# Attention and a gated feed-forward on one core: the written-out orders of 32 rounds replaced, with whole-quad exponentials

## The chip, the cores and the metric

The kernel runs on one core of a Trainium2 chip. The metric is the device time of one execution in microseconds (us); before the change it is 1197.77 us, the median of three runs (1197.53 to 1202.79). Engines are named as in the profile: PE is TensorE (matmuls), PEld its loading of weights, DVE is VectorE, ACT is ScalarE, POOL is GpSimd, SP is SyncE, which only issues transfers here.

## The reference

With S = 2048 tokens, D = 448, 16 heads of 28 and F = 1792, all in float32:

```python
qkv = x @ wqkv                                    # q, k, v of 16 heads
p = softmax(q @ k.T * 28 ** -0.5)                 # 2048 x 2048 a head
a = (p @ v) @ wo
gate, up = x @ W_gate, x @ W_up
b = (gate * (gate > 0) * up) @ W_down
g = sigmoid((x * gate_w).sum(-1, keepdims=True))
out = g * a + (1 - g) * b
```

## The kernel before

All orders of instructions are written out by hand. Each engine runs its own instructions in the order in which the program issues them; semaphores hold it where data or a buffer is missing.

There are three stages. The first (to about 137 us) projects x to q, k and v, spills q and k to DRAM and takes the first row maxima. The last (from about 1008 us) projects the attention's output with wo, runs the down projection and combines both. Between them lie 32 *rounds*, the loop at line 740: round v works on head v // 2 and half v % 2 of its keys. The lists of matmuls of the feed-forward's gate and up projections run through the rounds as filler.

A round is a string, one letter for one step, and the loop issues the steps in the order of the letters (lines 745 to 807). The letters are:

- **s**, `score()`, line 298: two matmuls (L306) of keys by queries into a wide PSUM tile of 2 x 512, and one ACT operation that empties it. For half of the 16 pairs of a round (after round 0) the score is final and ACT takes the exponential (L310). For the other half, the *raw* ones, the maximum of these queries isn't known yet: ACT copies the score, negated, to SBUF (L312), and the pair is noted in `todo_max`.
- **b**, `block_min()`, line 240: one DVE minimum (L256) over a raw pair, read from its PSUM tile and the running minimum of its block; the first one of a block reads the copy of the first pair and the tile of the second. Three of them finish a block (512 queries by 1024 keys, two blocks a round).
- **A**, `all_max()`, line 267: DVE reduces a finished block's minimum over the partitions (L271, L265, L275) and spreads it again (L279, `rm`).
- **g**, `take_max()`, line 282: POOL subtracts `rm` from one raw *quad* of 2048 elements a partition (L285); four a round.
- **e**, `take_exp()`, line 288: ACT takes the exponential of half a raw quad, 1024 elements (L296); eight a round. The dictionary `halves` remembers which half is next.
- **P** and **Q**, `pv()`, line 645: the product of the round's probabilities with v, 32 matmuls each on a tile of 32 columns (L653). P needs the first half of the round's keys, Q the second. After Q of an even round ACT copies the sum (L659), after Q of an odd one DVE adds to it (L661), and the row sums are sent to be inverted.
- **m**, `smax()`, line 190: two matmuls (L200) for the row maxima of a head to come, and a DVE reduction (L204) that empties the tile. **n**, line 208, turns a head's maxima into a row of Q (L212 and after).
- **x**: one matmul (L600) of the gate or up projection; 11 make a unit, and after a unit ACT takes the relu (L610) or DVE multiplies and SP stores (L613, L619).
- **w**: ACT and POOL split half of a gate/up weight tile in a high and a low part; SP loads the next.
- **c**, **f**: in odd rounds the two parts of `rescale()` (line 627), with DVE, ACT and POOL (L637, L640, L641). **N**: `normalise()` (line 677), POOL's multiplication with the inverted sums of the head before (L679) and four stores on SP. **D**: the split of a down-projection tile in the last rounds. **l**, **u**: once, in round 0.

s, m and n also start transfers and small steps: the first and the ninth s of an even round load k and q of a later head, the sixth calls `small_things` (lines 746 to 751).

s and m take their wide PSUM tiles in turn from three (`ps_w`, line 110): the fourth fill needs the first tile empty, that is the copy or exponential done, for raw pairs but the first of a block also the minimum, for m the reduction. The probabilities live in ten quads of SBUF (`NP`), and four pairs of the next round are scored ahead.

Before the change the list is `FIRST, A1`, then `Ee, Oe` three times, `A8`, then `O, E` ten times, and `L5, L6, L7`; E-type strings stand in even rounds, O-type in odd ones.

Of the kernel before, what the change touches and what calls it, by code (L numbers as in the profile page):

```python
# [42 lines left out]

NP = 10

FIRST = "sbbsbAxxxxlusxgxsxxsxssxsxxxsxxsesxxxxbegxxseexwPbbAQ"

A1 = "smsxxxswbxxxsgbsbnxxxxxssxssxxsAxemxwxmgxsmxxmcessxxxsmxsxbxeggxxxxxesebxeefbewxmmNAwPQ"

Ee = "gswmwsxxxxbsxgsxsxxbebxxxsxxssxxAxssxxemxxxmxsmxeexgmxxsexmxmxxsemxxxsgsbesbbewAwPQ"  # L50

Oe = "sgmgwsxxxxbssxxxsxbxxbxnsxsxsxsAwsxmxxemxxsmxeemsegwxmxxxxmsmxxgexNxsxsbesbxexbcwefxPAQ"

A8 = "wwwsmsxxsxxxxbsxbxgsexxsbxxxxsssxxgxxsAxmxmexxsxemxxgxmsxmexxmsxmxexxgessbbesPewbAQ"

O = "ssbnsxxxxsxbxNxbxxggsxxxxsxxxsxsxxssxxAmxsxxemsxmxexxmxsmxxemmgexsbxxxsbcxxxsbxAxmgeePefeQ"

E = "gsmsxxxxssebxxbbxxxsxxxxmxAexxssxgsxxsxxsxxmxxsxxemsmexgxexmxxxmsxmxexsbxsgebsebAPQ"

L5 = "sxsbNxxssxbxbxxxnxxxgssxxxegxxxAsxxsxgsxsxsxxxxxscsesxxxgxxxxxexxxxxeexsxeexxxsebbbfxxPAQ"  # L60

L6 = "DsxxsgxxxbsbxxgxssxxsxbexexxsAssxsxxxssxxxxexxxxgsgxxxexxxsxssexxebxexDbbxxxexPAQ"

L7 = "ssssxxxxxbxgxbxxxebxxxxxxgxxesxAxsexexxsgsxxxsxxxxgsxxxxxexesNexexxxcxDsxxxPfDQ"

ROUNDS = [
    FIRST, A1, Ee, Oe, Ee, Oe, Ee, Oe,
    A8, O, E, O, E, O, E, O,
    E, O, E, O, E, O, E, O,
    E, O, E, O, E, L5, L6, L7,  # L70
]


# [11 lines left out]
def gated_mix_kernel(ctx, tc, x, wq, wo, wgu, wd, out):  # L85
# [8 lines left out]
    def f32(ap):  # L94
        return ap.bitcast(F32)
# [21 lines left out]
    def ps_x(name):  # L117
        return psum.tile([P, TB], F32, tag="x", bufs=2, name=name)
# [71 lines left out]
    def smax(k):  # L190

        h, u, half = maxima[k]
        full = 4 * rows_of(h).count(2)
        if u == 0 and half == 0:
            MX[h] = keep.tile([P, 2 * full], F32, name=f"mx_{h}", tag="mx", bufs=2)
            M[h] = keep.tile([P, NU[h]], F32, name=f"m_{h}", tag="m", bufs=2)
        ps = ps_w(f"sm_{k}")
        for c in range(2):
            k0 = (half * 2 + c) * TB
            nc.tensor.matmul(ps[:, c, :], Q[h][:, u * P:(u + 1) * P], K[h % 3][:, k0:k0 + TB],  # L200
                             start=True, stop=True)
        c = 2 * u + half
        to = MX[h][:, c:c + 1] if u < full else M[h][:, u:u + 1]
        nc.vector.tensor_reduce(to, ps, axis=AX.XY, op=OP.max)  # L204
        if c == 2 * full - 1:
            nc.vector.tensor_reduce(M[h][:, :full], MX.pop(h).rearrange("p (a b) -> p a b", b=2), axis=AX.X, op=OP.max)
# [12 lines left out]
    AT, QUAD, slots = {}, {}, iter(range(10 ** 6))  # L219
# [18 lines left out]
    RM, R2, left = {}, {}, {}  # L238
# [46 lines left out]
        nc.gpsimd.tensor_tensor(QUAD[q], QUAD[q], m, op=OP.subtract)  # L285
        todo_exp.append(q)

    def take_exp():
        q = min(todo_exp, key=lambda q: (q[0], q[2], -q[1]))
        k = halves.pop(q, 0)  # L290
        if k:
            todo_exp.remove(q)
        else:
            halves[q] = 1
        q = QUAD[q][:, 2 * k:2 * k + 2].rearrange("p c t -> p (c t)")
        nc.scalar.activation(q, q, AF.Exp, scale=-SCALE)  # L296

    def score():

        v, done, q, half, chunks = stream.pop(0)  # L300
        h = v // 2
        if q not in QUAD:
            QUAD[q] = p_slot(next(slots) % NP, f"P_{v}_{q[1]}_{q[2]}")
        ps = ps_w(f"s_{v}_{chunks[0][0]}_{chunks[0][1]}")
        for c, (k, j) in enumerate(chunks):
            nc.tensor.matmul(ps[:, c], K[h % 3][:, k * P:(k + 1) * P], Q[h][:, j * TB:(j + 1) * TB], start=True, stop=True)  # L306
            AT[v, k, j] = QUAD[q][:, 2 * half + c]
        dst = QUAD[q][:, 2 * half:2 * half + 2]
        if done:
            nc.scalar.activation(dst, ps, AF.Exp, scale=SCALE)  # L310
        else:
            nc.scalar.activation(dst, ps, AF.Copy, scale=-1.0)  # L312
            todo_max.append((v, chunks[0][1], dst, ps if v else None))
# [275 lines left out]
    def load_f(i):  # L589
        if NF <= i < NB * NF:  # L590
            WS[i] = fe.tile([P, 2, 7, P], F32R, name=f"wg_{i}", tag="wg", bufs=2)
            nc.sync.dma_start(f32(WS[i]), ws_d[i % NF])
# [103 lines left out]
    def early_d():  # L696

        for i in range(0, 4, 2):
            h = fe.tile([P, 2, 4, P], F32, name=f"hk_{i}", tag="wgr", bufs=2).rearrange("p s c f -> p (s c f)")
            for k in range(2):  # L700
                DR[i + k] = V[:, 0].rearrange("p k h d -> p (k h d)")[:, (i + k) * D:(i + k + 1) * D]
                HK[i + k] = h[:, k * TB:(k + 1) * TB]
                nc.sync.dma_start(DR[i + k], wd[(i + k) * P:(i + k + 1) * P])
                nc.sync.dma_start(HK[i + k], h_d[i + k])
# [13 lines left out]
    def small_things(u):  # L718

        h, q = divmod(u, 4)  # L720

        if u in (22, 38):
            g = 2 if u < 32 else 3
            nc.sync.dma_start(V[:, g % 2], v_d[g])
        if u == 1:
            gates()
        if u == 2:
            pack_wo()
        if h and q == 1:
            row_sums(h - 1)  # L730
            spread(h - 1)

    def loads(h, load):

        if 2 < h + 2 < H:
            load(h + 2)
# [3 lines left out]
    for v, order in enumerate(ROUNDS):  # L740
        small_things(2 * v)
        if v == 2 * H - 3:
            early_d()
        ns = 0
        for o in order:
            if o == "s":
                ns += 1
                if ns == 6:
                    small_things(2 * v + 1)
                if ns in (1, 9) and v % 2 == 0:  # L750
                    loads(v // 2, load_k if ns == 1 else load_q)
                if stream:
                    score()
            elif o == "m":
                if m < len(maxima):
                    smax(m)
                    m += 1
            elif o == "x":
                i, half, n = passes.pop(0)
                if n == 0:  # L760
                    units.append((i, half, ps_x(f"gu_{i}_{half}")))
                gu_mm(units[-1][2], i, half, n)
                if n == NT - 1:
                    i, half, ps = units.pop()
                    if half:
                        finished.add(i)
                        load_f(i + 2)
                    spill_h(i, ps) if half else relu(i, ps)
            elif o == "n":
                if v % 2 and v < 2 * H - 1:  # L770
                    smax_end(v // 2 + 1)
            elif o == "w":
                ready = -(-starts[v + 2] // NT)
                ready = min(ready + ready % 2, 2 * NF)
                while parts < ready and (parts < 4 or parts // 2 - 2 in finished):
                    split_f(parts // 2, act_high, pool_low, (parts % 2,))
                    parts += 1
                    if parts % 2 == 0:
                        fetch_f(parts // 2 + 1)
            elif o == "b":  # L780
                block_min()
            elif o == "A":
                all_max()
            elif o == "g":
                take_max()
            elif o == "N":
                if v > 1 and v % 2:
                    normalise(v // 2 - 1)
            elif o == "e":
                take_exp()  # L790
            elif o in "cf":
                rescale(v, "cf".index(o))
            elif o == "D":
                split_wd(len(early))
                early.append(o)
            elif o == "l":
                sends.pop()()
            elif o == "u":
                split_f(0, act_high, pool_low, (1,))
                QS.append(last_q("Q2"))  # L800
                for a, b in ((GD, 12), (GD + 12, 4)):
                    nc.sync.dma_start(f32(QS[2])[a:a + b].rearrange("p j t -> p (j t)"), Q[1][GD + 2:GD + 2 + b].bitcast(F32))
                load_q(2)
                fetch_f(2)
                parts = 2
            elif o in "PQ":
                pv(v, "PQ".index(o))
        rest = [k for k in todo_exp + todo_sub + todo_all if k[0] == v]
        assert not rest and v not in PO or len(stream) == max(0, 16 * (2 * H - 1 - v) - AHEAD), (v, passes, rest, len(stream) + 16 * (v + 1))
# [178 lines left out]
```

## Time and profile before

| | us |
|---|---|
| median of three runs | 1197.77 |
| lowest and highest | 1197.53, 1202.79 |
| span of the profiled execution (first to last instruction) | 1198.9 |
| granted TensorE clock | 1.000 |

The profiled execution's own time isn't given beside its span; the span is 1.1 us above the median.

| stretch, us | PE | DVE | ACT | POOL |
|---|---|---|---|---|
| 207.80 to 235.32 (one early round) | 27.31 | 24.23 | 26.06 | 23.12 |
| 371.43 to 923.47 (20 rounds) | 552.02 | 488.28 | 484.73 | 401.31 |
| 923.47 to 949.58 | 25.94 | 16.52 | 23.11 | 19.16 |
| 949.58 to 976.61 | 25.41 | 15.32 | 25.38 | 21.83 |
| 1047 to 1199 | 148.27 | 55.43 | 32.87 | 23.37 |

How to read it: busy times are unions of the instructions' spans on an engine. Matmuls are pipelined and their ends are modelled, so PE counts as busy in short waits too; what it lost is seen in the chain that ended last, where its pieces have start and length. A group of instructions has its line, engine, operation, output and input with their shapes, the count, then busy time and mean ns of one, then the idle time of the engine just before them and what ended it.

### The profile page before, as it was taken

Reading aid. Unit: us, or ns where it says so; the run is one execution under the profiler, and the core shown is the slowest. Engines: PE = TensorE matmul, PEld = TensorE weight load, DVE = VectorE, ACT = ScalarE, POOL = GpSimd, SP = SyncE. Lnnn points to the kernel's source line nnn. Section 1 sums busy time; section 2 is a strip of 40 time slices with the busy share of each in tenths; the row PEclk is TensorE's granted clock in tenths of the full one; section 3 lists DMA queues with packets and bytes.
Section 4 is the critical chain, followed back from the end, with each engine's and each line's share of the span. In section 5 each row is a group of like instructions: output and inputs, shape, how many; then the busy total and the mean of one; then the engine's idle time right before and its main releaser. Section 6 shows DMA issues by size and latency. Waiting matters only on the chain.

```text
span 1198.9 us, 16948 instructions
## 1 busy us (share of the span) xinstructions
PE 1183.7 (99%) x6183; PEld 820.1 (68%) x6183; DVE 902.8 (75%) x1179; ACT 878.2 (73%) x1082; POOL 748.9 (62%) x326
## 2 busy tenths in 40 slices
PE   9999999999999999999999999999999999999998
PEld 6888755556656666666666666666666666899997
DVE  6466798888898989898888989898988653544242
ACT  5321789999999888888788888888888896422121
POOL 4222387889897777766676767777767786522020
PEclk9999999999999999999999999999999999999999
DMA  9956354354535453443536443436443425743342
GB/s 317 319 207 250 136 191 137 111 141 143 156 129 159 148 163 114 124 122 117 150 119 186 118 129 110 128 117 191 112 126 105 138 89 161 218 136 119 114 128 75
DMA packets 63486, 178.35 MB, mean 149 GB/s; under 512 B 13050, under 2 KB 19650, under 8 KB 58754
## 3 DMA queue, kind: packets, MB, share of 16 engines
q1 hardware_dynamic: 56812, 151.53, 41.1%
q0 software_dynamic: 6160, 25.30, 5.5%
q8 instruction: 48, 0.79, 0.3%
q10 hardware_dynamic: 432, 0.46, 0.1%
q14 instruction: 34, 0.28, 0.1%
HBM read 118.58 MB, written 58.87 MB: 148 GB/s over the span
## 4 chain that ended last, share of the span: by engine, by line
PE 85%; DVE 5%; ACT 3%; DMA 3%; issue 1%; POOL 1%; SPq 1%; DVEq 0%; POOLq 0%; ACTq 0%
PE gu L600 19%; PE s L306 18%; PE po L653 18%; PE sm L200 10%; PE acc L893 10%; PE qk L427 6%; PE wo L852 3%; PE v L445 3%; DVE r L256 1%; ACT P L310 1%; DVE mx L204 1%; ACT P L312 1%; ACT P L296 1%; DMA ls<-os 1%; DMA wor<-wo_d 1%
## 5 line engine op out<-in xcount | busy, mean ns | idle before, releaser
L285 POOL TENSOR_TENSOR P<-P,rm 128x2048 f32<-128x2048 f32 x102 | 470.7, 4633 | 95.5 <-DVE rm L279 79.7
L600 PE MATMUL gu<-X,wg 128*128 128x512 f32 x1232 | 364.6, 395 | 0.7 <-ACT rl L610 0.7
L204 DVE TENSOR_REDUCE mx<-sm 128x1 f32<-128x1024 f32 x256 | 301.5, 1215 | 40.9 <-PE sm L200 40.5
L306 PE MATMUL s<-Q,K 128*128 128x512 f32 x1024 | 316.8, 405 | 6.2 <-ACT V L310 1.9
L600 PEld LDWEIGHTS gu<-X,wg 128*128 128x128 f32 x1232 | 231.2, 188 | 56.7 <-ACT rl L610 2.0
L306 PEld LDWEIGHTS s<-Q,K 128*128 128x128 f32 x1024 | 178.1, 188 | 98.5 <-DVE mn L265 13.4
L312 ACT ACTIVATE P<-s 128x1024 f32<-128x1024 f32 x204 | 202.9, 1031 | 44.2 <-PE s L306 41.6
L653 PE MATMUL po<-P,V 128*32 128x512 f32 x1640 | 227.7, 594 | 0.4 <-ACT P L296 0.4
L296 ACT ACTIVATE P<-P 128x1024 f32<-128x1024 f32 x204 | 213.2, 1072 | 2.1 <-POOL P L285 1.8
L310 ACT ACTIVATE P<-s 128x1024 f32<-128x1024 f32 x206 | 201.5, 1039 | 9.0 <-PE s L306 7.7
L256 DVE SCALAR_TENSOR_TENSOR r<-s,r 128x1024 f32<-128x1024 f32 x124 | 151.6, 1223 | 19.0 <-ACT P L312 10.5
L200 PE MATMUL sm<-K,Q 128*128 128x512 f32 x520 | 163.7, 399 | 0.7 <-DVE mx L204 0.6
L653 PEld LDWEIGHTS po<-P,V 128*32 128x32 f32 x1640 | 63.5, 110 | 116.3 <-issue 108.8
L653 PE MATMUL po<-V 128*32 128x512 f32 x408 | 135.9, 594 | 0.0
L285 POOL TENSOR_TENSOR V<-V,rm 128x2048 f32<-128x2048 f32 x24 | 111.1, 4634 | 23.0 <-DVE rm L279 19.3
L121 ACT ACTIVATE hh<-hr 128x512 fp32r<-128x512 f32 x52 | 32.8, 631 | 117.9 <-PE acc L893 111.8
L200 PEld LDWEIGHTS sm<-K,Q 128*128 128x128 f32 x520 | 91.3, 188 | 33.2 <-ACT P L310 5.6
L127 DVE TENSOR_TENSOR hh<-hr,hh 128x512 fp32r<-128x512 f32 x52 | 47.8, 926 | 82.6 <-ACT hh L121 78.9
L893 PE MATMUL acc<-WD,hh 128*128 128x448 f32 x480 | 100.7, 368 | 0.0
L893 PEld LDWEIGHTS acc<-WD,hh 128*128 128x128 f32 x480 | 90.1, 188 | 8.8
L256 DVE SCALAR_TENSOR_TENSOR r<-s,P 128x1024 f32<-128x1024 f32 x50 | 61.1, 1223 | 38.3 <-ACT P L312 38.3
L271 DVE TRANSPOSE_TENSOR_REDUCE mn<-r 128x32 f32<-128x1024 f32 x63 | 78.0, 1238 | 1.3
(87 smaller groups left out, 1142.6 us busy)
## 6 DMA issues: line engine op xcount, KB each, us to landing
wg<-ws_d SPq DMA_DIRECT2D x42, 896.0 KB
K<-qk_d SPq DMA_DIRECT2D x32, 448.0 KB
Q<-qk_d SPq DMA_DIRECT2D x64, 224.0 KB
h_d<-h SPq DMA_DIRECT2D x56, 256.0 KB
hr<-h_d SPq DMA_DIRECT2D x52, 256.0 KB
ws_d<-wg SPq DMA_DIRECT2D x14, 896.0 KB
qk_d<-st POOLq DMA_DIRECT2D x21, 512.0 KB, 3.2
wgr<-wgu SPq DMA_DIRECT2D x13, 512.0 KB
```

The costliest lines, as they stand in the source:

```text
L200: nc.tensor.matmul(ps[:, c, :], Q[h][:, u * P:(u + 1) * P], K[h % 3][:, k0:k0 + TB], start=True, stop=True)
L204: nc.vector.tensor_reduce(to, ps, axis=AX.XY, op=OP.max)
L256: nc.vector.scalar_tensor_tensor(r, ps, -1.0, before, op0=OP.mult, op1=OP.min)
L271: nc.vector.tensor_reduce(MN[:, 1:3], R2.pop((v, j)).rearrange("p a (b r) -> p a b r", r=32), axis=AX.X, op=OP.min, apply_transpose=True)
L285: nc.gpsimd.tensor_tensor(QUAD[q], QUAD[q], m, op=OP.subtract)
L296: nc.scalar.activation(q, q, AF.Exp, scale=-SCALE)
L306: nc.tensor.matmul(ps[:, c], K[h % 3][:, k * P:(k + 1) * P], Q[h][:, j * TB:(j + 1) * TB], start=True, stop=True)
L310: nc.scalar.activation(dst, ps, AF.Exp, scale=SCALE)
L312: nc.scalar.activation(dst, ps, AF.Copy, scale=-1.0)
L600: nc.tensor.matmul(ps, WS[i][:, s, a], xf(i // NF, b), start=(n == 0), stop=(n == NT - 1))
L653: nc.tensor.matmul(po[32 * j:32 * j + 32], V[:, h // 4 % 2, k, h % 4], AT.pop((v, k, j)), start=(k == k0), stop=(k == k0 + NK // 2 - 1))
L893: nc.tensor.matmul(ACC[i // NF][t][:, :D], HH[i][:, a, t * P:(t + 1) * P], wd_high_low(f, b), start=(f == 0 and n == 0), stop=(f == NF - 1 ...
```

## The change

The sixteen orders R0 to R12 and R29 to R31 replace the ten before. Round 0 keeps its string. Rounds 1 to 8 get an order each; rounds 9 to 28 repeat R9, R10, R11, R12; the last three are new. A new letter E takes the exponential of a whole raw quad in one ACT operation of 2048 elements; e still takes half. In the list of rounds each b stands later behind the s of its pair than before, on the mean.

```diff
@@ -43,31 +43,43 @@
 
 NP = 10
 
-FIRST = "sbbsbAxxxxlusxgxsxxsxssxsxxxsxxsesxxxxbegxxseexwPbbAQ"
-
-A1 = "smsxxxswbxxxsgbsbnxxxxxssxssxxsAxemxwxmgxsmxxmcessxxxsmxsxbxeggxxxxxesebxeefbewxmmNAwPQ"
-
-Ee = "gswmwsxxxxbsxgsxsxxbebxxxsxxssxxAxssxxemxxxmxsmxeexgmxxsexmxmxxsemxxxsgsbesbbewAwPQ"
-
-Oe = "sgmgwsxxxxbssxxxsxbxxbxnsxsxsxsAwsxmxxemxxsmxeemsegwxmxxxxmsmxxgexNxsxsbesbxexbcwefxPAQ"
-
-A8 = "wwwsmsxxsxxxxbsxbxgsexxsbxxxxsssxxgxxsAxmxmexxsxemxxgxmsxmexxmsxmxexxgessbbesPewbAQ"
-
-O = "ssbnsxxxxsxbxNxbxxggsxxxxsxxxsxsxxssxxAmxsxxemsxmxexxmxsmxxemmgexsbxxxsbcxxxsbxAxmgeePefeQ"
-
-E = "gsmsxxxxssebxxbbxxxsxxxxmxAexxssxgsxxsxxsxxmxxsxxemsmexgxexmxxxmsxmxexsbxsgebsebAPQ"
-
-L5 = "sxsbNxxssxbxbxxxnxxxgssxxxegxxxAsxxsxgsxsxsxxxxxscsesxxxgxxxxxexxxxxeexsxeexxxsebbbfxxPAQ"
-
-L6 = "DsxxsgxxxbsbxxgxssxxsxbexexxsAssxsxxxssxxxxexxxxgsgxxxexxxsxssexxebxexDbbxxxexPAQ"
-
-L7 = "ssssxxxxxbxgxbxxxebxxxxxxgxxesxAxsexexxsgsxxxsxxxxgsxxxxxexesNexexxxcxDsxxxPfDQ"
+R0 = "sbbsbAxxxxlusxgxsxxsxssxsxxxsxxsesxxxxbegxxseexwPbbAQ"
+
+R1 = "smNsxsxbxsxwbxbwnxxgsxxxwxsgAwxsxssxxsxsmxExxmxxmxxssxgxmsxxbsbcxexxxexmsPbgAmEemfexQ"
+
+R2 = "gwsmsxsxbxswxxxxxxbExbxsxsxxmAxsxsxsxgxxxsmxxsxmExmgsxxgmxxsxmxExsssewxbbePwbmAQ"
+
+R3 = "smgsxsxbxwxbswxxxsxxxxsbxwAxsswxxxggsmnxgxsxemxsmxxssmxexEmxxxmxxsbxNxssxEebbcePfAmxQ"
+
+R4 = "gwsmsxxsxbsxxxxxbexwxsbxssmxsgAxxssxxsxmxsexxxmgsmxxxxmmgwsxxxEExxsexxsbxmebbAPwQ"
+
+R5 = "smsxsxggxxsxwbbxbnxAsxxxxsxssxsxwsxEwmxxgmxxmxsxxxxsmsExmxxmsxxxesxsNcbbegebfAPemwxxQ"
+
+R6 = "smsxxbgsxsxxxwbxxsxbwxssssAgxsxmxxxsxxmxExmxsxxmsgEmxxmxxxEgxxmxssxsbPbewxbexwAQ"
+
+R7 = "ngsmsxxxssNxbxxxsxxxwbbxsxxsssxwsexxAxmxxxmswgxxsxgmsxmexgmsxxsebbxxxsxxemPEbecfeAxmQw"
+
+R8 = "swmssxbxwxxsbxbxxsxxsgxwExxxmsxmxsxxxgAsxxssxmsxxmxsemxxmsxgxExgxxsbxmbsbeeewxAPQ"
+
+R9 = "nsmsbxxxgsxxbsbxxxsxxxxsxxgsxxAsxxsmsNxxxsmsxxsmsxxsxxxxbbxmxxEmgxxEgsxxxmbxcEAeexfxmPQ"
+
+R10 = "smsxxgxxssbbbxxxxxxExxmxsxxsxxxsxxAsxxxsmsxxxgsmsxEmxxmggsxExmxxmsxsbxxexbsebAPQ"
+
+R11 = "nsmsbxxxsxbxxsxbxxAxsgxxsgxxssxxsxsxgxmxsxxmxsmxxxEmxsxmExExmxxmxxxNcxxxsgssbbefxxebPAQ"
+
+R12 = "smsbgxxxxssxxxxxsbxxxxbAxxessxgxsxsxxsxmxexxmxsmxxsmxxmgxEmsgxxxxmxxEssxebbsePbQA"
+
+R29 = "NgsxsbsxbxxxxsbnxxsxxxsxAxxxExxgxxsxsgsxsxxxxxsxxxsxxxxsxEsbExxsgxcxesxxxxexxfbPbAQ"
+
+R30 = "DsxxsxsxxsgxxxbsxbxbxxsxxxxEAxgsxgsxxxxxsxxxsxxsxsxxxssxExxbxsxxxEgxsexxxDexxbxxbPQA"
+
+R31 = "sxNxsbxsxxgxxxbssxxxxbxsxAxexsxsexgxxExxxxxxgxsexxgxxxexsxxsxxcexxexsDfDPxQ"
 
 ROUNDS = [
-    FIRST, A1, Ee, Oe, Ee, Oe, Ee, Oe,
-    A8, O, E, O, E, O, E, O,
-    E, O, E, O, E, O, E, O,
-    E, O, E, O, E, L5, L6, L7,
+    R0, R1, R2, R3, R4, R5, R6, R7,
+    R8, R9, R10, R11, R12, R9, R10, R11,
+    R12, R9, R10, R11, R12, R9, R10, R11,
+    R12, R9, R10, R11, R12, R29, R30, R31,
 ]
 
 
@@ -285,14 +297,14 @@
         nc.gpsimd.tensor_tensor(QUAD[q], QUAD[q], m, op=OP.subtract)
         todo_exp.append(q)
 
-    def take_exp():
+    def take_exp(whole):
         q = min(todo_exp, key=lambda q: (q[0], q[2], -q[1]))
         k = halves.pop(q, 0)
-        if k:
+        if k or whole:
             todo_exp.remove(q)
         else:
             halves[q] = 1
-        q = QUAD[q][:, 2 * k:2 * k + 2].rearrange("p c t -> p (c t)")
+        q = QUAD[q][:, 2 * k:4 if whole else 2 * k + 2].rearrange("p c t -> p (c t)")
         nc.scalar.activation(q, q, AF.Exp, scale=-SCALE)
 
     def score():
@@ -786,8 +798,8 @@
             elif o == "N":
                 if v > 1 and v % 2:
                     normalise(v // 2 - 1)
-            elif o == "e":
-                take_exp()
+            elif o in "eE":
+                take_exp(o == "E")
             elif o in "cf":
                 rescale(v, "cf".index(o))
             elif o == "D":
```

## The prediction

> **What bounds the kernel now.** I read the page first: the busy shares, then the chain that ended last.
>
> ```profile
> span 1198.9 us, 16948 instructions
> ...
> PE 1183.7 (99%) x6183; PEld 820.1 (68%) x6183; DVE 902.8 (75%) x1179; ACT 878.2 (73%) x1082; POOL 748.9 (62%) x326
> ...
> PE 85%; DVE 5%; ACT 3%; DMA 3%; issue 1%; POOL 1%; SPq 1%; DVEq 0%; POOLq 0%; ACTq 0%
> ```
>
> TensorE looks full, but the ends of matmuls are modelled, so a matmul that waits a little for its PSUM tile still counts as busy. The question is therefore how much of the span TensorE would need if no matmul waited. For that I read the chain in order of time, at whole P-V blocks (po, 64 instructions), which come once a round, and the times of undisturbed matmuls between them.
>
> ```profile
> 180.07 7.00 PE po L653 x64
> ...
> 371.43 7.00 PE po L653 x64
> ...
> 923.47 7.00 PE po L653 x64
> ...
> 943.99 3.27 PE gu L600 x14
> ...
> 949.58 7.27 PE po L653 x64
> ...
> 976.61 7.30 PE po L653 x64
> ```
>
> ```profile
> 574.78 0.92 PE s L306 x4
> ...
> 599.23 1.14 PE s L306 x4
> 600.37 0.11 PE mt L212
> ```
>
> A 512-column matmul takes 3.27/14 = 0.233 us, a round's P-V block 7.00. The four matmuls straight behind a block take 1.14 instead of 0.92: the turn from a block to other work costs 0.2 us, whatever the order. The first and the last block, and the end, are read from the timeline of TensorE:
>
> ```profile
> 149.11 3.83 PE L653 MATMUL po<-P,V 128*32 128x512 f32 x31
> ...
> 1000.85 5.44 PE L653 MATMUL po<-P,V 128*32 128x512 f32 x48
> ...
> 1007.41 0.60 PE L653 MATMUL po<-P,V 128*32 128x512 f32 x2
> ...
> 1046.42 0.68 PE L852 MATMUL wo<-WO,on 128*128 128x448 f32 x2 [1.76 <-POOL on L130]
> ```
>
> Now count letters between one block and the next (s and m are two matmuls, x is one, and the mt of 0.11 comes every second round) and subtract.
>
> Block 0 to 1: 81 matmuls and a block are 18.9 + 7.0 = 25.9; it took 180.07 - 149.11 = 31.0. **Lost 5.1.**
> Blocks 1 to 8: 7 x (25.9 + 0.06) = 181.5; it took 191.4. **Lost 9.9**, of it 7 x 0.2 = 1.4 for the turns.
> Blocks 8 to 28: ten pairs of 88 and 85 matmuls, 54.4 a pair, 544.2; it took 552.0. **Lost 7.8**, of it 4.0 for the turns.
> Blocks 28 to 31: 79 + 73 + 68 = 220 matmuls, 51.3 + 21 = 72.3; it took 77.4. **Lost 5.1**, of it 0.6 for the turns.
> After block 31 TensorE runs on and waits once, 1.76 us ahead of the output projection.
>
> So an order without any wait could save about 4.9 + 8.5 + 3.8 + 4.5 + 1.8 = 23.5 us, and no order more. What holds TensorE is the three wide PSUM tiles that s and m share: the fourth fill waits until ScalarE or VectorE has emptied the first. How full those are:
>
> ```profile
> 235.32:262.38 27.06, 26.76 (x149) 16.61 (x153) 24.88 (x34) 25.12 (x31) 25.14 (x12) 1.00 0.55 151
> 262.38:289.97 27.59, 27.35 (x150) 16.33 (x154) 24.23 (x32) 26.25 (x35) 22.67 (x10) 1.00 0.35 126
> ...
> 371.43:923.47 552.04, 552.02 (x3025) 353.30 (x3028) 488.28 (x645) 484.73 (x550) 401.31 (x123) 1.00 0.44 132
> ```
>
> (In the view by windows the columns are the length, then PE, PEld, DVE, ACT, POOL.) In the early rounds ScalarE works 25.1 to 26.3 of 27.1 to 27.6 us, as much as TensorE needs (25.9): two engines of equal load and a third (VectorE, 24.2 to 24.9) close behind. From round 9 on the shares are 88% for both, and the loss is small.
>
> **The change, part by part.** TensorE's work is the same: each letter but e occurs as often as before in the whole list, and 79 E take the place of 158 e. Three x leave round 29 and three leave round 31, six go to round 30.
>
> *Whole exponentials.* Their price comes from these groups:
>
> ```profile
> L310 ACT ACTIVATE P<-s 128x1024 f32<-128x1024 f32 x206 | 201.5, 1039 | 9.0 <-PE s L306 7.7
> L296 ACT ACTIVATE P<-P 128x1024 f32<-128x1024 f32 x204 | 213.2, 1072 | 2.1 <-POOL P L285 1.8
> L256 DVE SCALAR_TENSOR_TENSOR r<-s,P 128x1024 f32<-128x1024 f32 x50 | 61.1, 1223 | 38.3 <-ACT P L312 38.3
> L121 ACT ACTIVATE hh<-hr 128x512 fp32r<-128x512 f32 x52 | 32.8, 631 | 117.9 <-PE acc L893 111.8
> L121 ACT ACTIVATE WO<-wor 128x1344 fp32r<-128x1344 f32 x1 | 1.3, 1309 | 0.0
> ```
>
> From 512 to 1344 elements an ACTIVATE grows by (1309 - 631)/832 = 0.815 ns an element, so one of 2048 is estimated at 1072 + 1024 x 0.815 = 1.91 us. No trace here shows one. Against two halves that is 0.24 us less; where ScalarE runs without a gap two halves take only 1.89 (the row x2 below), and the saving is 2 x 0.945 - (0.945 + 0.835) = 0.11. So 0.11 to 0.24 per E: 79 E free 9 to 19 us of ScalarE, 17 E in rounds 1 to 8 two to four. The Trainium skill (ScalarE: Activation LUTs, What ACT_TABLE_LOAD costs) gives an ACTIVATE with immediate operands 186 ns and 0.833 ns an element, back-to-back ones overlapping by 93 ns; by that each E would free 0.09 to 0.19 us, 7 to 15 in all, and the halves' 1072 here lie 33 ns above its figure. It counts on TensorE only where ScalarE is what it waits for.
>
> ```profile
> 144.08 4.24 DVE e L556
> 148.63 4.25 DVE gate L558
> ...
> 300.05 1.72 ACT P L312 x2
> ...
> 304.80 3.76 ACT P L310 x4
> ...
> 310.90 1.89 ACT P L296 x2
> 312.79 0.93 ACT V L310
> ```
>
> That is so in the early even rounds: this chain stays on ScalarE from 300.05 to 313.72, because the repeated order piles four half exponentials onto the copies.
>
> *Minima behind their copies.* The row of r<-s,P shows VectorE standing 38.3 us before 50 minima, waiting for ScalarE's copy, with the maxima (m) queued behind. By the letters a minimum follows its fill by 0.47 us of TensorE work in rounds 9 to 28, less than the 1.04 of the copy; in the new orders by 0.82, in rounds 1 to 8 by 1.42 instead of 1.03. So VectorE does maxima in that time and frees m's tiles earlier. Against it, the tile of the copied pair is held as long as before. Worth between nothing and the waits of m's tiles, which are part of the losses above.
>
> *Own orders, rounds 1 to 8.* Block 0 to 1: the gates' two operations of 4.24 and 4.25 us on VectorE stand in round 0, which keeps its order, so I take 1.0 of 4.9. Blocks 1 to 8: between none and all of 8.5; I take half, 4.2, because ScalarE's load stays near TensorE's. Rounds 1 to 3 and 5 to 7 put m or x between P and Q: the last exponentials get time, but each makes one more turn, 6 x 0.2 = 1.2. Net 3.0.
>
> *Rounds 9 to 28.* Half of 3.8: 1.9.
>
> *Rounds 29 to 31.* The chain shows both minima in the way:
>
> ```profile
> 957.61 1.95 ACT P L312 x2
> ...
> 959.59 1.24 DVE r L256
> ...
> 962.19 0.73 PE s L306 x2
> ...
> 1003.24 1.25 POOL os L679
> ...
> 1007.43 1.29 POOL os L641
> ...
> 1008.74 0.70 DVE os L661
> ```
>
> Round 30 now has 79 matmuls instead of 73 ahead of its block and ScalarE has 3 E in each of 29 and 30: I take 2.5 of 4.5. In round 31 N stood behind the last subtraction, so the normalisation of head 14 (1.25) ran ahead of the rescaling (1007.43) for which head 15's addition (1008.74) waited. Now N comes third. The addition can then start at the end of Q, 1008.0: 0.7 us, all of it inside the 1.76 that TensorE waits later.
>
> *Queues.* N moves also its four stores on SP, w its weight loads, the sixth and ninth s their loads of Q and V. The DMA share of rounds 9 to 28 is 0.44, which covers them; a late load of gate/up weights would cost one unit's wait, under 2 us.
>
> **Sum.** 1.0 + 3.0 + 1.9 + 2.5 + 0.7 = 9.1 us. The profiled span is 1198.9, already 1.1 above the median of 1197.77 (the page gives no more of its own time), so the difference is taken from the median: **1188.7 us**.
>
> **Rivals.** *All waits go:* 23.5 - 1.2 = 22.3, 1175.5. For it: every loss is a wait for a tile, and no engine alone exceeds 26.3 us a round. Against: three engines at 90 to 97% in the early rounds would have to fit without a gap. Between it and the forecast lies 1176 to 1182; chance 0.11.
>
> *The waits only move:* the early rounds are set by ScalarE and VectorE together, and a smoother order runs into the other queue; the gain of rounds 1 to 8 is eaten by the extra turns, rounds 9 to 28 give nothing, and half of the last rounds' 3.2 remains: 1196. Chance 0.24.
>
> *E holds up the copies, slower:* ScalarE works in order, so a copy behind an E starts up to 1.91 - 1.07 = 0.84 later. It decides where the copy's tile is refilled within 1.91 + 1.04 = 2.95 us of the E; by the letters that is so at 3 of 79, by 0.2 us each, if ScalarE comes to the E without a backlog. With the backlog of 300 to 314 it is so at each of the 17 E of rounds 1 to 8: +14.3, against 5.1 from the other rounds: 1207. The Trainium skill (TensorE: Matmul & The Clock Gate, Architectural detail) calls ScalarE's queue strict first-in first-out, eight deep, while TensorE may only pull weight loads ahead; by that rule no copy gets past an E. The trace agrees, the chain of ACT above being in the order of the letters. Chance 0.13.
>
> **How the numbers follow.** Forecast 0.52, all waits gone 0.11, moved 0.24, held up 0.13. A measurement here can tell 0.5%, 6 us: faster below 1191.8, slower above 1203.8. Faster 0.52 + 0.11 = 0.63, same 0.24, slower 0.13. The range reaches down to the bound of the sum, 1176, and up through most of "moved" to 1200, leaving out what lies in "held up".
>
> **What would show it.** Blocks 0 to 8 (the blocks themselves move by a few letters) in 218 us instead of 222.3, 8 to 28 in 550, 28 to 31 in 75, the output projection's wait near 1.0; L296 with 79 instructions of about 1.9 us; VectorE's idle time before r<-s,P well below 38. The forecast is wrong if rounds 1 to 8 don't shorten (then ScalarE's load, not its order, bounds them), or if s waits for ACT behind a whole exponential.

## The result, and the profile after

The changed kernel takes 1212.26 us (median of four runs, 1210.45 to 1216.61), the one before 1197.85 beside it: ratio 1.0118, 95% interval 1.009 to 1.0145. It is **slower by 14 us**, 1.2%; the prediction was 1188.7, with 1176 to 1200 as its range. The profiled execution took 1211.34 us, its span is 1209.6. Of the runs below, one execution of e9 (1445.76 us) and one of e15 (4134.21 us) were far slower than the others of their kernels; they are in no ratio, and their profiles are not used.

The page of the profile after, beside the rows of before in the prediction:

```profile
span 1209.6 us, 16837 instructions
...
PE 1188.0 (98%) x6183; PEld 824.0 (68%) x6183; DVE 912.5 (75%) x1179; ACT 878.1 (73%) x1003; POOL 749.3 (62%) x326
...
PE 85%; DVE 6%; DMA 4%; ACT 2%; issue 1%; POOL 1%; SPq 1%; DVEq 0%; POOLq 0%; ACTq 0%
...
L268 DVE SCALAR_TENSOR_TENSOR r<-s,P 128x1024 f32<-128x1024 f32 x50 | 61.1, 1223 | 31.2 <-ACT P L324 31.0
```

ScalarE has 79 instructions fewer and the same busy time (878.1 after 878.2), and of the chain's shares DMA's grew from 3% to 4% and DVE's from 5% to 6%, while ACT's fell from 3% to 2%. One per cent is 12 us, about the size of the difference, but the shares are whole per cents and don't say which of them it is. Where the time went is read from the chain in order of time, at the same P-V blocks as before (block k is the one of round k; line numbers after are those of before plus 12):

```profile
180.11 3.57 PE po L665 x32
...
376.66 7.00 PE po L665 x64
397.78 5.71 DMA X<-x_d
407.04 7.00 PE po L665 x64
...
600.10 7.00 PE po L665 x64
621.71 5.77 DMA X<-x_d
631.04 7.00 PE po L665 x64
...
845.66 5.13 DMA X<-x_d
...
936.80 7.00 PE po L665 x64
```

The chain of before had no piece of DMA between blocks 8 and 28. Now a load of X stands in three rounds, 9, 17 and 25, and those last 30.4, 30.9 and 30.3 us from block to block (407.04 - 376.66 is the first), while the same string takes 28.2 in rounds 13 and 21. The first and last blocks, from TensorE's timeline:

```profile
148.77 1.54 PE L665 MATMUL po<-P,V 128*32 128x512 f32 x11
...
1013.36 3.21 PE L665 MATMUL po<-P,V 128*32 128x512 f32 x28 [0.96 <-ACT rl L622]
...
1058.76 0.67 PE L864 MATMUL wo<-WO,on 128*128 128x448 f32 x2 [1.08 <-POOL on L142]
```

| us, profiled execution | before | after | forecast |
|---|---|---|---|
| blocks 0 to 8 | 222.3 | 227.9 | 218 |
| blocks 8 to 28 | 552.0 | 560.1 | 550 |
| blocks 28 to 31 | 77.4 | 76.6 | 75 |
| block 31 to the end | 198.1 | 196.2 | 197.3 |
| wait of the output projection | 1.76 | 1.08 | near 1.0 |

The spans differ by 10.7 us: -0.3 up to block 0, +5.6 in the early rounds, +8.1 in the steady ones, -0.8 in the last and -1.8 after them. (The medians differ by 14.4: beside the span there are 1.7 us in the profiled execution, which lies 0.9 below its median, while the span of before lies 1.1 above its own.) Both kernels have 648 matmuls of s, m and x between blocks 0 and 8, and equally many between 8 and 28; the last three rounds have one fewer. What stands behind block 31 differs from run to run: in other profiles with the same last rounds it took 195.5 to 201.3 us, so the -1.8 there says little.

### The profile page after: what moved, and what is told of

It reads as the page before. It is cut to its first block, busy times and chain, and to the rows that moved or that the text cites. A ratio compares the mean times of both kernels' runs of the same rounds, so it can differ in the third digit from the quotient of the medians.

```text
span 1209.6 us, 16837 instructions
## 1 busy us (share of the span) xinstructions
PE 1188.0 (98%) x6183; PEld 824.0 (68%) x6183; DVE 912.5 (75%) x1179; ACT 878.1 (73%) x1003; POOL 749.3 (62%) x326
## 4 chain that ended last, share of the span: by engine, by line
PE 85%; DVE 6%; DMA 4%; ACT 2%; issue 1%; POOL 1%; SPq 1%; DVEq 0%; POOLq 0%; ACTq 0%
PE gu L612 19%; PE po L665 18%; PE s L318 17%; PE acc L905 10%; PE sm L212 9%; PE qk L439 6%; PE wo L864 3%; DVE r L268 3%; PE v L457 3%; DMA X<-x_d 1%; ACT P L324 1%; DMA l_d<-rq 1%; DMA or<-o_d 1%; DVE mx L216 1%; DMA ls<-os 1%
## 5 line engine op out<-in xcount | busy, mean ns | idle before, releaser
L216 DVE TENSOR_REDUCE mx<-sm 128x1 f32<-128x1024 f32 x256 | 305.4, 1218 | 54.7 <-PE sm L212 53.0
L318 PE MATMUL s<-Q,K 128*128 128x512 f32 x1024 | 321.8, 404 | 6.0 <-DVE mx L216 2.4
L318 PEld LDWEIGHTS s<-Q,K 128*128 128x128 f32 x1024 | 181.9, 188 | 86.8 <-DVE r L268 17.1
L308 ACT ACTIVATE P<-P 128x1024 f32<-128x1024 f32 (+1 forms) x140 | 201.8, 1459 | 2.0 <-POOL P L297 1.7
L268 DVE SCALAR_TENSOR_TENSOR r<-s,r 128x1024 f32<-128x1024 f32 x124 | 151.8, 1225 | 21.4 <-ACT P L324 10.2
L212 PEld LDWEIGHTS sm<-K,Q 128*128 128x128 f32 x520 | 93.8, 188 | 34.1 <-DVE mx L216 4.4
L268 DVE SCALAR_TENSOR_TENSOR r<-s,P 128x1024 f32<-128x1024 f32 x50 | 61.1, 1223 | 31.2 <-ACT P L324 31.0
```

The costliest lines, as they stand in the source:

```text
L268: nc.vector.scalar_tensor_tensor(r, ps, -1.0, before, op0=OP.mult, op1=OP.min)
```

## The experiments

The rows of before and after suggest a first theory. Here are TensorE's waits by what they wait for (total, times, longest), and around the first reload of X the queues of SP and POOL and TensorE's timeline, all after:

```profile
PE gu L612 <- DMA X<-x_d: 4.6, 6, 1.3
```

```profile
390.14 2.43 SPq L616 DMA_DIRECT2D X<-x_d  x4
394.69 1.61 SPq L693 DMA_DIRECT2D o_d<-os  x4
396.40 1.76 SPq L616 DMA_DIRECT2D X<-x_d  x4
```

```profile
384.19 9.22 POOL L297 TENSOR_TENSOR P<-P,rm 128x2048 f32<-128x2048 f32 x2
393.37 1.29 POOL L691 TENSOR_TENSOR os<-os,rb 128x512 f32<-128x512 f32 x1
```

```profile
403.54 0.73 PE L612 MATMUL gu<-X,wg 128*128 128x512 f32 x2 [1.29 <-DMA X<-x_d]
```

The tokens that the feed-forward works on change three times, at x number 308, 616 and 924, each the 22nd x of an R9, and X is then loaded anew in eight transfers (L616). N stands in the middle of them. Its four stores (L693) wait on SP for POOL's multiplication (L691), which waits for two subtractions of 4.6 us that were issued ahead of it. SP issues in order, so the last four loads of X wait as well: 2.1 us from 392.57 to 394.69 with nothing issued, then 1.6 for the stores. Before, N came earlier, POOL was free for it, and the loads went out in one piece behind the stores:

```profile
383.36 1.70 SPq L681 DMA_DIRECT2D o_d<-os  x4
385.17 4.30 SPq L604 DMA_DIRECT2D X<-x_d  x8
```

**Theory Q**: transfers held up on SP cost most of the loss. **Rival E**: the whole exponentials hold up copies. **Rival O**: the new orders are slower in themselves, by waits for tiles.

The ratios below are against all executions of the kernel before that had been collected by then (medians 1198.87 to 1200.28), so equal times of two runs needn't have equal ratios.

### N behind the reload; whole exponentials as halves

e1 moves one letter of R9, e2 replaces E by ee in every string.

```diff
-R9 = "...smsNxxxsmsxxsmsx..."
+R9 = "...smsxxxsmsxNxsmsx..."
```

```diff
-R2 = "...mxEx...", and so on
+R2 = "...mxeex...", and so on
```

> The changed kernel with the N of R9 moved seven letters later, behind the 22nd x, so that all eight transfers that reload X are issued ahead of the four stores of the normalisation. Theory 'SP queue' (stores wait for POOL until 393.4 and hold the second half of the reload): rounds 9, 17 and 25 fall from 30.4, 30.9 and 30.3 us between blocks to the 28.2 of rounds 13 and 21, the kernel from 1212 to about 1205. Rival 'slow landing' (the letters between last and next use, 4.4 to 6.5 us, are too few for 5.2 us of transfer in any order): these rounds stay above 29.5, the kernel above 1209.

> The changed kernel with each E written as ee, two half exponentials at the same place. Theory 'E holds up the copies': faster by 5 us or more, 1207 or less. Theory 'SP queue': the exponentials' size is not what lost time; within 3 us of 1212, rather above it by what ScalarE loses in rounds 1 to 8 (17 times 0.1 to 0.24, 2 to 4 us).

e1: 1206.68 us, ratio 1.0046 (1.0024 to 1.0068): by the ratios one letter takes back 0.7 of the 1.2%, by the medians 5.6 of the 14.4 us. Its profiled execution ran at a clock of 0.949, so its blocks are compared with each other, an R9 without a reload (488.30) and one with it (600.23), in its chain:

```profile
488.30 7.32 PE po L665 x64
516.81 7.32 PE po L665 x64
...
600.23 7.32 PE po L665 x64
628.72 7.32 PE po L665 x48
```

28.51 and 28.49: the reload now costs nothing. e2: 1212.95, 1.0107 (1.007 to 1.0144), no different from the change. The interval is wide, but the traces agree: blocks 1 to 8, where E was to hold up the copies at 17 places, take 196.5 us with E and with ee. So E is no cause, and no gain that these runs can show, though its price was as estimated (after, groups of one shape):

```profile
L308 ACT ACTIVATE P<-P 128x2048 f32<-128x2048 f32 x64 | 122.1, 1918 | 0.1
```

### The parts of the change alone; the cause put into the kernel before

e3, e4 and e5 take from the change only rounds 9 to 28, 1 to 8 and 29 to 31. e7 is the kernel before with N moved into the reload:

```diff
-O = "ssbnsxxxxsxbxNxbxxggsxxxxsxxxsxsxxss..."
+O = "ssbnsxxxxsxbxxbxxggsxxxxsxxxsxsxNxss..."
```

> The kernel before with R9 to R12 in rounds 9 to 28, and its own orders elsewhere. Theory 'SP queue': three reloads at 2.2 to 2.8 each, plus 1 for the rest: 1197.9 + 8 = 1206. If the loss were the new early rounds' late start that runs through the steady ones: 1199 or less.

> The kernel before with R1 to R8 in rounds 1 to 8, and its own orders elsewhere. By the traces blocks 0 to 8 take 227.8 instead of 222.3: 1197.9 + 5.5 = 1203.4. If the parts didn't add (backlog handed over to rounds 9 and on): above 1206.

> The kernel before with R29 to R31 in its last three rounds. By the traces blocks 28 to 31 take 76.6 instead of 77.5 and TensorE's wait ahead of the output projection 1.1 instead of 1.8: 1 to 2 us faster than the kernel before, 1196 to 1197. The prediction's term for it was 3.2.

> The kernel before with one letter moved: the N of its odd order O goes from behind the 6th x to behind the 18th, between the first four and the last four transfers that reload X in rounds 9, 17 and 25. Theory 'SP queue': these three rounds lengthen by 1.5 to 3 us each, the kernel by 5 to 9; rounds 11, 13, 15 and so on, which have the same N and no reload, stay within 0.3. Rival 'slow landing' or any other property of the new orders: no change.

| kernel | us | ratio (interval) | blocks 0-8 | 8-28 | 28-31 |
|---|---|---|---|---|---|
| e3, rounds 9 to 28 | 1207.68 | 1.0067 (1.0046 to 1.0089) | 222.0 | 559.0 | 77.4 |
| e4, rounds 1 to 8 | 1205.59 | 1.0045 (1.0028 to 1.0062) | 225.9 | 553.6 | 77.5 |
| e5, rounds 29 to 31 | 1198.71 | 0.9996 (0.9984 to 1.0009) | 222.2 | 552.3 | 76.7 |
| e7, before with N in the reload | 1210.59 | 1.0098 (1.0068 to 1.0129) | 222.3 | 563.2 | 77.5 |

The three parts add up: 0.67% + 0.45% - 0.04% is 1.08%, against 1.18% for all. (In e4, 1.5 us of the 553.6 are a wait for X in round 9.) And e7 makes the kernel before slower by nearly as much, with no new order at all. Its SP queue and its waits:

```profile
384.71 2.26 SPq L604 DMA_DIRECT2D X<-x_d  x4
390.96 1.61 SPq L681 DMA_DIRECT2D o_d<-os  x4
392.67 1.76 SPq L604 DMA_DIRECT2D X<-x_d  x4
```

```profile
PE gu L600 <- DMA X<-x_d: 7.1, 3, 3.1
```

Here SP stood 4.0 us. Rounds 9, 17 and 25 took 30.5, 32.7 and 31.6 instead of 28.0; the other odd rounds kept their 27.9 to 28.4. That is 11.2 us for blocks 8 to 28, more than the 5 to 9 expected: in rounds 17 and 25 the granted clock was 0.50 for 3.4 us behind the wait for X (619.8 to 623.2 and 845.1 to 848.4), which costs 1.7 us each time, and without that it is 7.8. For the reloads theory Q is shown from both sides.

### The early rounds: loads of Q and the row sums

In an even round the sixth s issues the row sums (VectorE's reciprocal, L680, a store of it, four loads that spread it) and the ninth s the load of Q behind them, all on SP. In the new strings both stand closer to heavy transfers. After (round 4):

```profile
250.19 0.34 SPq L597 DMA_DIRECT2D ws_d<-wg  x1
...
253.42 0.45 SPq L681 DMA_DIRECT2D l_d<-rq  x1
261.49 2.19 SPq L687 DMA_DIRECT2D rb<-l_d  x4
...
264.41 3.36 SPq L187 DMA_DIRECT2D Q<-qk_d  x4
```

```profile
271.94 0.70 PE L212 MATMUL sm<-K,Q 128*128 128x512 f32 x2 [0.80 <-DMA Q<-qk_d]
```

```profile
307.90 0.25 DVE L680 RECIPROCAL rq<-ls 128x16 f32<-128x16 f32 x1 [1.87 <-DMA ls<-os]
```

The store of the row sums is small, but SP could read it back only 8.07 us later (261.49 - 253.42). The spill of the feed-forward weights (896 KB, 250.19) and other loads were under way: from 253.5 to 257.0 the DMA engines were 0.95 busy. Before, it took 2.81, at a busy share of 0.44 (250 to 253):

```profile
250.07 0.38 SPq L669 DMA_DIRECT2D l_d<-rq  x1
252.88 1.71 SPq L675 DMA_DIRECT2D rb<-l_d  x4
```

That the traffic is the reason is read from these rows; no run changes it alone.

Either way, Q came late for the maxima of round 5. In round 6 VectorE stood 1.87 us for the row sums, with A queued behind. e6 is e1 with Q loaded ahead of the row sums; e8 issues the row sums at the ninth s, e9 at the eleventh:

```diff
-                if ns == 6:
-                    small_things(2 * v + 1)
-                if ns in (1, 9) and v % 2 == 0:
+                if ns in (1, 6) and v % 2 == 0:
                     loads(v // 2, load_k if ns == 1 else load_q)
+                if ns == 6:    # e8: 9, e9: 11
+                    small_things(2 * v + 1)
```

> e1_n_behind with the load of q issued at the sixth s of an even round, ahead of the row sums' store and the loads that wait for it, instead of at the ninth. Theory 'q behind the sums on SP': the maxima of round 5 no longer wait until 271.9, blocks 4 to 5 fall by 1 to 2 us, blocks 0 to 8 from about 226 to 224 or 225; round 6, where VectorE's reciprocal waits for the row sums' transfer, keeps its 30.0. Rival 'compute order': blocks 0 to 8 within 0.5 of 226.

> As e6_q_first, with the row sums' step (VectorE's reciprocal and its transfers) moved from the sixth to the ninth s of an even round. Theory 'reciprocal ahead of the block's minimum in VectorE's queue, its transfer behind 896 KB of weights': VectorE no longer waits 1.9 us at the reciprocal in round 6, blocks 5 to 6 fall from 30.0 to 28 or less and blocks 0 to 8 by 2 to 4 us against e6_q_first, the kernel to about 1201. Rival 'compute order': blocks 5 to 6 stay above 29.5.

> As e8_sums_later, with the row sums' step at the eleventh s. In R6 the sixth to the ninth s follow each other straight ahead of A, so e8 left the reciprocal ahead of the block's minimum there; the eleventh stands behind A in every even round. Theory 'reciprocal ahead of the block's minimum': VectorE's wait of 1.84 us for the row sums' transfer is gone in round 6, blocks 5 to 6 fall from 29.9 to 28.2 or less, blocks 0 to 8 from 225.5 to 223.5. Rival 'compute order': blocks 5 to 6 stay above 29.5.

| kernel | us | ratio (interval) | block 4-5 | block 5-6 | 8-28 |
|---|---|---|---|---|---|
| after | 1212.26 | 1.0118 (1.009 to 1.0145) | 27.7 | 30.0 | 560.1 |
| e6 | 1205.81 | 1.0048 (1.0025 to 1.0071) | 26.7 | 29.9 | 555.2 |
| e8 | 1204.90 | 1.0050 (1.0033 to 1.0067) | 26.7 | 29.9 | 553.4 |
| e9 | 1205.06 | 1.0043 (1.0027 to 1.0058) | | | |

Q in time gains 1 us in round 5; e8 left round 6 as it was, since there the ninth s still stands ahead of A. e12 below contains the same edit as e9, and in its trace the reciprocal runs behind A (310.19) without a wait. Block 5 to 6 then takes 28.8 instead of 29.9, where 28.2 or less was expected. Yet the medians of e1, e6, e8 and e9 can't be told apart: by the blocks, each mend is worth 1 us. With TensorE's waits for transfers gone (e8) the steady rounds are at 553.4 against 552.0 of before: theory Q explains 6.7 of the 8.1 us there, and the other 1.4 stay open.

### What is left in rounds 4 to 8

In e12 blocks 1 to 8 still take 194.5 us against 191.4 before, with 5 matmuls more (1.2 us): 2 us are left, mostly in rounds 4, 6 and 8. POOL stood 2.59 us in round 5 for ScalarE's exponential of the letter f. e15 (e18 is the same kernel again, for its profile) puts f two letters earlier, e16 puts w ahead of f; both on e9, e15 with the gates of e13 below.

```diff
-R5 = "...NcbbegebfAPemwxxQ"
+R5 = "...NcbbefgebAPemwxxQ"      # e15, e18
+R5 = "...NcbbegebwfAPemxxQ"      # e16
```

> The new orders with N behind the reload, Q loaded at the 6th s and the row sums at the 11th (as in e9), the gates' other form (as in e13), and in round 5 the letter f two letters earlier: ...cbbefgeb... instead of ...cbbegebf.... In e12 POOL stood 2.59 us for ScalarE's exponential of f in round 5, ahead of the split of the feed-forward weights. Theory (POOL's wait is the rest): that wait goes below 0.7 us, blocks 4 to 8 fall from 26.7 + 28.8 + 27.1 + 28.4 = 111.1 (e12) to 109.5 or less. Rival (ScalarE's and VectorE's load is the rest): POOL's wait goes, but blocks 4 to 8 stay within 0.6 of 111.1. Time by the theory about 1201, by the rival 1203.

> The same kernel as e15, for its profile. If ScalarE's exponential of f now waits for the transposed differences of c (VectorE behind two minima, POOL behind the normalisation), ScalarE stands for some us in round 5 and block 4 to 5 or 5 to 6 is 5 us or more longer than in e12 (26.7 and 28.8). If instead no block is longer by more than 1 us, the 8 us were the clock.

> e9 (the new orders with N behind the reload, Q at the 6th s, row sums at the 11th) with the letter w of round 5 ahead of f: ...bebgebwfAPemxxQ instead of ...bebgebfAPemwxxQ. POOL then splits the feed-forward weights before it comes to the multiplication for which it waited 2.59 us for ScalarE in e12. Theory (POOL's wait delays the weights' spill and all that stands behind it on SP): block 5 to 6 falls from 28.8 (e12) to 28.2 or less and blocks 4 to 8 from 111.1 to 110.4 or less. Rival (the load of ScalarE and VectorE): blocks 4 to 8 stay within 0.5 of 111.1. Time 1204 or 1205.

e15: 1214.43, 1.0121 (1.0099 to 1.0144); e18: 1216.29, one run. My theory fell, and the block 5 to 6 of 37.1 us shows how. In e18, POOL, then ScalarE, then TensorE:

```profile
294.95 1.28 POOL L655 TENSOR_TENSOR os<-os,rs 64x512 f32<-64x512 f32 x1 [6.40 <-ACT rs L654]
```

```profile
300.84 2.00 ACT L308 ACTIVATE P<-P 128x1024 f32<-128x1024 f32 x2 [6.03 <-POOL P L297]
```

```profile
301.95 1.07 PE L667 MATMUL po<-P,V 128*32 128x512 f32 x2 [5.43 <-ACT P L308]
```

f now stands ahead of g, so POOL's multiplication, which needs ScalarE, stands ahead of POOL's last subtraction of the round. POOL waited 6.40 instead of 2.59, the last exponentials waited for it, and TensorE for them, 5.43 us; from 298.8, within that wait, the granted clock was 0.50 for 6.8 us. I had expected ScalarE to be the one that stands. e16: 1206.83, 1.0057 (1.0038 to 1.0076); POOL's wait for f is gone, but it now stands nearly as long (2.27 us) ahead of w, for matmuls that still read the weight tile, and blocks 4 to 8 take 111.9, no less than the 111.1 of e12.

So POOL's wait isn't what is left. The extra turns are of that size: in six of the new orders m or x stands between P and Q. In e12 (round 2):

```profile
208.11 3.57 PE po L665 x32
211.68 0.66 PE sm L212 x2
212.34 3.57 PE po L665 x32
```

The two halves and the two matmuls between them take 7.80 us (208.11 to 215.91), where a block in one piece and two matmuls take 7.00 + 0.47. That is 0.33 for the extra turn, and six of them are 2.0 us; the prediction had them at 0.2 each. No run puts these letters behind the block, so that nothing else is in the 2 us isn't shown.

### The gates, and the search for a version that beats both

Between blocks 0 and 1 the kernel before loses 4.9 us; just ahead of block 0 and in its beginning VectorE spends 4.24 and 4.25 us on two operations of 16 columns (quoted in the prediction). Nothing in the change touches them. e10 issues them earlier, ahead of POOL's subtractions; e13 writes them as additions with a tile of ones; e17 gives the additions to ScalarE, so that VectorE only inverts.

```diff
-        if u == 1:
+        if u == 0:                                            # e10, e11, e12
             gates()
...
-        nc.vector.tensor_scalar_add(e, e, 1.0)
+        nc.vector.tensor_tensor(e, e, ones, op=OP.add)        # e13, e14, e15, e18
...
+        nc.scalar.activation(e[:, 0], zt, AF.Exp, scale=-1.0) # e17
+        nc.scalar.activation(e[:, 1], zt, AF.Exp, scale=1.0)
+        nc.scalar.activation(e, e, AF.Copy, bias=1.0)
+        nc.vector.reciprocal(gate, e)
```

e11, e14 and e17 also have the new rounds 29 to 31, and e12 is e9 with e10's edit.

> The kernel before with the gates' step at the start of round 0 instead of its sixth s, so that it runs ahead of POOL's first subtraction. In the kernel before its two operations on 128x16 took 4.30 and 4.25 us and ended each with one of POOL's two subtractions. Theory 'they wait for POOL's long operation': they take under 1.5 us each, VectorE has up to 8 us more in round 0, block 0 to 1 falls from 30.9 to 27 to 28, the kernel by 2 to 4 us to about 1196. Rival 'these operations are that long': no change of either.

> The kernel before, with the gates' two VectorE operations of 16 columns in the same place in another form: tensor_tensor with a tile of ones (an addition and a subtraction) instead of tensor_scalar with constants. Theory (the form): a tensor_scalar of this kind doesn't run beside POOL's subtraction but a tensor_tensor does; then each takes under 0.7 us where the two took 4.30 and 4.25, the block before stays at 149.1 (in e10 it came at 152.9), block 0 to block 1 falls from 30.9 to about 29.0, and the time by 1 to 2 us: 0.999. Rival (the place): any VectorE operation there is held while POOL subtracts; both stay above 4 us, block 0 to block 1 stays at 30.9 and the time is the same.

> The kernel before with the new orders of rounds 29 to 31 (as e5), and the gates without VectorE's two held operations: ScalarE takes the exponentials of z and of -z and adds one to both, VectorE only inverts both (1/(1+exp(-z)) and 1/(1+exp(z))). Theory: the additions were held because a VectorE operation that reads two tiles of SBUF or runs as tensor_scalar can't run beside POOL's subtraction, while a reciprocal can (0.24 us beside POOL in other rounds). Then VectorE is free of 8 us, block 0 stays at 149, block 0 to block 1 falls from 30.9 to 29.0 as in e10, and with the last rounds the time is 2 to 3 us lower: 0.998 (0.997 to 0.999). Rival (the 8 us aren't what is waited for, or ScalarE's three small operations cost as much): block 0 to 1 stays above 30.4, ratio 0.9996 to 1.0003.

> e10_gates_first with R29 to R31 in the last three rounds: 0.5 to 1.5 us below e10_gates_first, if the gains add; by this the new last rounds are worth keeping.

> e13 with the new orders of rounds 29, 30 and 31. By the form theory the gain of e13 adds to the 0.8 us that blocks 28 to 31 gained in e5: 2 to 3 us below the kernel before, 0.998. If the form changes nothing, it is e5 again: 0.9996.

> e9_sums_11 with the gates at the start of round 0: block 0 to 1 from 29.8 to 26 to 27, the kernel 2 to 4 us below e9_sums_11. If the new orders have a gain of their own once transfers no longer hold them, this is below e10_gates_first; if they only lost by transfers and gain nothing else, it is within 3 us of it.

| kernel | us | ratio (interval) | block 0 at | block 0-1 |
|---|---|---|---|---|
| before | | | 149.1 | 30.9 |
| e10 | 1201.59 | 1.0022 (1.0008 to 1.0036) | 152.9 | 29.0 |
| e11 | 1201.37 | 1.0023 (1.0004 to 1.0042) | 153.0 | 29.5 |
| e13 | 1199.05 | 0.9995 (0.9984 to 1.0005) | 148.8 | 30.9 |
| e14 | 1200.72 | 1.0003 (0.999 to 1.0016) | 149.0 | 30.9 |
| e17 | 1200.03 | 0.9998 (0.9984 to 1.0012) | 149.6 | 30.8 |
| e12 | 1206.27 | 1.0056 (1.0034 to 1.0078) | 153.1 | 27.1 |

The operations themselves, in VectorE's timelines of e10, e13 and e17:

```profile
137.46 0.17 DVE L556 TENSOR_SCALAR e<-e 128x16 f32<-128x16 f32 x1 [1.93 <-ACT e L555]
...
137.96 0.59 DVE L558 TENSOR_SCALAR gate<-gate 128x16 f32<-128x16 f32 x1
```

```profile
143.74 4.31 DVE L558 TENSOR_TENSOR e<-e,ones 128x16 f32<-128x16 f32 x1
```

```profile
144.14 0.33 DVE L590 RECIPROCAL gate<-e 128x32 f32<-128x32 f32 x1
...
162.48 1.23 DVE L288 SCALAR_TENSOR_TENSOR r<-s,P 128x1024 f32<-128x1024 f32 x1 [2.37 <-ACT P L344]
```

Moved ahead of POOL's work they take 0.17 and 0.59, but TensorE then waits for what stands behind them, and block 0 comes 3.8 later. Of this, 2.05 are the wait below; behind it the granted clock was 0.50 from 147.7 to 151.1, which is another 1.7. e11 and e12 show the same wait and the same clock. In e10:

```profile
146.77 0.74 PE L600 MATMUL gu<-X,wg 128*128 128x512 f32 x2 [2.05 <-DVE pair L127]
```

In the other form they are held as before: my theory of the form fell. In e17 VectorE has 8 us less to do, and the stretch is no shorter. TensorE's wait before, and in e17:

```profile
161.55 0.73 PE L306 MATMUL s<-Q,K 128*128 128x512 f32 x2 [1.62 <-DVE mx L204]
```

```profile
163.76 0.73 PE L338 MATMUL s<-Q,K 128*128 128x512 f32 x2 [1.44 <-DVE r L288]
```

The wait for the maximum became one for a minimum, which itself stood 2.37 us for ScalarE's copy: ScalarE was the next in line. No version beat the kernel before; e5, e13, e14 and e17 equal it. e11 lies 0.2 us below e10 and e12 1.2 above e9, where gains of 0.5 to 1.5 and of 2 to 4 were expected.

## Why the prediction was wrong

**The step that failed** is the one on *Queues*: N's stores were costed at nothing, since "the DMA share of rounds 9 to 28 is 0.44, which covers them". A share says how busy the 16 engines are, not in what order SP issues. What decides is which instruction of SP stands behind one that waits for POOL. At three places these were the loads of X, and the price was 2.1 to 2.8 us each, where the text had "under 2 us", once, for gate/up weights. Together they are 7 of the 10.7 us by which the spans differ (e1 takes them away, e7 puts them into the kernel before). The position of N among the letters and the x at which X is reloaded were both to be counted in advance; I counted letters for tiles, not for transfers.

**Own orders, rounds 1 to 8**, taken as -3.0, with -1.0 for block 0 to 1: they gave +5.6 (e4 alone +3.7), partly by the same neglect (Q and the row sums on SP behind large transfers, 2 us mended), partly by a clock that dipped after a wait (below, 1.6), and the 2 us that are left are the size of the six extra turns, priced at 0.2 each and measured at 0.33. Beside these the new early orders gained nothing that can be seen, where 4.2 + 1.0 was expected. "I take half" of the loss had no row behind it: that the engines were 90 to 97% busy spoke for less.

**Rounds 9 to 28**, taken as -1.9: without the reload +1.4. Moving each minimum behind its copy did shorten VectorE's idle time before the 50 minima, 38.3 to 31.2 over the whole kernel, not "well below", while that before the other 124 (r<-s,r on the pages) grew from 19.0 to 21.4; no gain of TensorE is seen in these rounds.

**Rounds 29 to 31**, taken as -2.5: -0.8, of it 0.2 for the missing matmul; right in sign, three times too large. **N in round 31**, -0.7: the output projection's wait fell by 0.68, as worked out, but by luck of this execution. In e5, with the same last rounds, it was 1.97, where 1.1 was expected, and in other runs with them 1.1 to 2.7; before it was 1.76. A gain from N isn't shown, and e5 as a whole equals the kernel before (0.9996, interval 0.9984 to 1.0009).

**E**: 1.91 was estimated and 1.92 measured, and no gain from it can be seen (e2). The rival that E holds up the copies named 1207, near the result, by a mechanism that e2 speaks against. "The waits only move" described the rounds themselves best, but no rival held the transfers. The accounting of TensorE's lost time holds: the same matmuls and the same 0.233 us. The difference is in waits, and beside them in the extra turns and in the clock.

## What to carry to other kernels

Where steps are reordered, list for each transfer queue what it will issue and in what order, and look at each entry that waits for a compute engine: what is queued behind it, and when is that needed? A low DMA share says nothing about that. And a long operation that goes away gains nothing until the engine that is next in line has been found: twice here (e10, e17) the wait only changed its name. And a block of matmuls that is split in two has a price of its own, to be read from a row before the order is written.

## What the runs showed of the hardware

Some of VectorE's small operations on SBUF waited for a whole POOL operation: the gates' took 4.30 and 4.25 us as tensor_scalar and 4.31 as an addition of two tiles while POOL subtracted (4.6 each), and 0.17 and 0.59 when it didn't. Reciprocals of 16 and 32 columns were not held (0.25 at 307.90 after, 0.33 in e17, both while POOL subtracted). The Trainium skill (SBUF — State Buffer, Who interferes with whom) says that a VectorE instruction in a two-port mode, which tensor_scalar can enter, contends with GpSimd for a shared pair of ports that whichever issues first holds for its whole instruction, and that one with two SBUF inputs contends with a GpSimd instruction that reads SBUF. The traces of before, e10 and e13 agree with it, and by it e13's form could not have helped.

The granted clock of TensorE fell behind some of its waits. After, it waited 2.11 us for the maximum ahead of 161.17, e4 2.12 at the same place, e10 2.05 ahead of 146.77. By windows (the clock is the third number from the end), after, e4 and e10:

```profile
162.20:165.50 3.30, 3.30 (x10) 2.36 (x9) 2.35 (x3) 2.11 (x3) 3.30 (x2) 0.50 1.02 416
```

```profile
162.20:165.50 3.30, 3.30 (x17) 2.58 (x15) 2.38 (x3) 3.01 (x5) 3.30 (x2) 1.00 1.02 411
```

```profile
147.70:151.10 3.40, 3.40 (x10) 2.63 (x9) 0.17 (x1) 2.25 (x3) 3.40 (x2) 0.50 0.94 369
```

The clock is halved from 1.9 to 3.6 us behind the start of the wait, for 3.4 us (6.8 in three cases), which costs 1.7 us where TensorE works all the time: block 0 to 1 took 31.3 after, but 29.7 in e4, with the same string. The same wait of 2.1 us brought this in one execution and not in another. In the traces of before, after and e2 to e18 (without e9 and e15), between 20 us after the start and 20 us before the end, no wait of TensorE between 0.9 and 1.92 us was followed by a halved clock, 8 of 15 between 1.94 and 2.19 were, and 6 of 7 of 2.6 or more; no halved clock stood there without such a wait. The wait ahead of the maximum is 1.62 us in the kernel before and 2.11 in the changed one, so the new early orders brought it to where this can happen. The four executions of the changed kernel were granted 0.996 to 0.999 of the clock; 0.0025 of 1212 us is 3 us, so by this estimate some 3 of the 14 us are the clock. A new wait of about 2 us can thus cost nearly twice its length, and the loss differs from one execution to the next.
